# A long convolution with a gated mix on one Trainium2 core: the inverse stage in eight 32x64 array tiles, two channels side by side in the first exchange, and a rewritten order

## The chip, the cores and the metric

The kernel runs on one core of a Trainium2 chip. The core has a matrix engine (TensorE, PE in the rows), a vector engine (VectorE, DVE), a scalar engine (ScalarE, ACT), a general engine (GpSimd, POOL) and an engine that only issues transfers here (SyncE, SP). Each engine works through its own instructions in program order and waits at semaphores for the others. PE writes to PSUM, from which DVE and ACT read; all other working data lie in SBUF.

The metric is device time in microseconds (us). The kernel before takes 198.89 us, the median of 3 runs between 198.06 and 199.80.

## What is computed

The input is one sequence of 2048 tokens with 512 channels, all in fp32. Two branches are mixed by a gate per token:

```python
k_shift = sum(k_pad[:, t:t + S, :] * shift_k[:, ks - 1 - t] for t in range(4))   # 4 taps per channel
kv = k_shift * v
y = irfft(rfft(kv padded to 2S) * rfft(ssm_k padded to 2S))[:S] + kv * ssm_D     # long causal convolution
a = q * y
r = q @ w_r; idx = top2(r)                                                       # two routed tokens
ffn = (silu(q[idx] @ w_gate) * (q[idx] @ w_up)) @ w_down * sigmoid(r[idx])
b = q; b[idx] += ffn
g = sigmoid((q * gate_w).sum(-1))
out = g * a + (1 - g) * b
```

## The kernel before

The 512 channels are worked in four chunks `c` of 128. For each chunk the convolution is a transform of length 2048 = 64 x 32, done by matmuls against constant tables, and these are the stages:

- `taps(c, x)`: the four taps of a quarter of the chunk's tokens, multiplied and added in SBUF tile `acc` (4 buffers). ACT makes the first product. The other three are done on DVE for the four blocks of chunk 0 (`TAPS_DVE`), elsewhere by a product on ACT (`tap`) and an addition on POOL.
- `T(c, x)`: four PE transposes into PSUM tile `ps` (one buffer), and a DVE product with `v` into `kv`.
- `A(c, b)` and `C(c, b)`: matmuls with `w1` over 64 positions, of the filter `hN` and of `kv`, into a PSUM tile `p2`. There are three `p2` buffers, of two banks each, which `A`, `C`, `S` and `I` share. `exchange` (line 149) then has DVE transpose the 128x1024 tile in 32x32 blocks out of PSUM into `e`. A chunk has eight of these. `skip` (`D` in the order) adds one row to `hN` on POOL before `A`.
- `S(c, u)`, eight a chunk: 16 matmuls with `w2` into `p2`, on eight array tiles of 64 rows by 32 columns; ACT copies one half to `g`; DVE makes the products `y1` and `y2`; after every second `S`, POOL adds or subtracts their halves. `y1` and `y2` have two buffers.
- `I(c, u)`, four a chunk: the inverse with `w3`, four matmuls of 64x128 tiles and 512 columns in two row halves, into one `p2`; two ACT copies of 128x512 put it into `f`.
- `X(c, i)`, four a chunk: DVE transposes `f` in place in 32x32 blocks, when all of the chunk's `I` are there.
- `J(c, mb)`, four a chunk: eight matmuls with `vv`, into `ps`, or into `p2` for the last chunk; then the gate (`gcol`, `omg`), four small instructions on ACT or DVE as `GATE` says; then a product with `q` (`qN`, 4 buffers) on POOL or DVE; then the store.
- `G`: the steps of `ffn`, that is the gate and router over all tokens, the search for two tokens, and their feed-forward matmuls, whose weights stream through `wff` (two buffers). `Z(c)` scatters the routed result with an addition, issued by POOL.

Each fp32 matmul is recorded as two instructions. The names `L...` in the order are loads, all issued by SP. The string `ORDER` sets everything: every name in it runs its function up to the next `yield`, so the string is the program order of all engines at once.

Of the kernel before, what the change touches and what calls it, by code (L numbers as in the profile page):

```python
# [519 lines left out]
```

## Time and profile before

| | before |
|---|---|
| median of 3 runs | 198.89 us |
| the profiled execution | 198.09 us |
| its span, first to last instruction | 196.1 us |
| PE busy | 146.9 us (75%) |
| DVE busy | 150.6 us (77%) |
| ACT busy | 93.3 us (48%) |
| POOL busy | 115.4 us (59%) |
| moved by DMA | 39.77 MB, mean 203 GB/s |

The profile is of one execution. Busy time is the union of an engine's instructions, without issue and semaphore time, and a group's mean is the length of one instruction, of which several can overlap on PE. PE's weight loads (PEld) have their own column. The idle time before a group is put down to what released its last instruction.

### The profile page before, as it was taken

To read this page: it belongs to the slowest core of one execution; us is meant where nothing else is said; L and a number is where in the kernel's file an instruction comes from. 1 tells how busy PE (TensorE), PEld (TensorE's weight loads), DVE (VectorE), ACT (ScalarE), POOL (GpSimd) and SP (SyncE) were. 2 spreads that over 40 slices of the span, in tenths; PEclk is the share of its full clock that TensorE was granted. 3 is DMA by queue.
4 is the path that set the end of the run, shared out by engine and by line. 5 is a ranking of instruction groups with operands and counts; after the bars stand their busy time and mean duration, and the time that the engine had idled before them with its cause. 6 is when DMAs were issued, how large, how long until landed. Compare 5 with 4: busy or idle time off the path is not lost. (4 is left out here: it accounts for less than half of the span.)

```text
span 196.1 us, 4562 instructions
## 1 busy us (share of the span) xinstructions
PE 146.9 (75%) x1822; PEld 70.3 (36%) x1822; DVE 150.6 (77%) x179; ACT 93.3 (48%) x178; POOL 115.4 (59%) x107
## 2 busy tenths in 40 slices
PE   0028748788978797998897999899989997974700
PEld 0014222334523234542443534444356452423600
DVE  0198799997889998999769879988999845047540
ACT  0611655265597245753395672432556555660500
POOL 0021889159899276974595898460613992931662
PEclk9999999999999999999999999999999999998885
DMA  5999994858699300079578464675640757786140
GB/s 133 366 324 273 341 341 166 295 196 310 210 322 349 119 0 4 3 246 336 194 271 278 159 230 142 208 232 174 187 149 24 261 140 242 184 275 209 60 159 0
DMA packets 16473, 39.77 MB, mean 203 GB/s; under 512 B 2361, under 2 KB 2883, under 8 KB 16325
## 3 DMA queue, kind: packets, MB, share of 16 engines
q1 hardware_dynamic: 16292, 39.48, 60.7%
q8 instruction: 14, 0.23, 0.5%
q0 software_dynamic: 160, 0.01, 0.2%
q14 instruction: 7, 0.05, 0.1%
HBM read 35.28 MB, written 4.20 MB: 201 GB/s over the span
## 5 line engine op out<-in xcount | busy, mean ns | idle before, releaser
L149 DVE STREAM_TRANSPOSE e<-p 128x1024 f32<-128x1024 f32 x32 | 62.8, 2041 | 5.6 <-PE p L199 2.9
L229 POOL TENSOR_TENSOR y<-y 128x512 f32<-128x512 f32 x32 | 40.3, 1282 | 21.6 <-DVE y L222 21.3
L176 POOL TENSOR_TENSOR acc<-acc,tap 128x512 f32<-128x512 f32 x36 | 45.9, 1280 | 11.1 <-ACT tap L174 6.7
L212 PE MATMUL p<-e,w 64*32 64x256 f32 x1024 | 32.7, 380 | 5.9 <-DVE e L149 5.1
L241 PE MATMUL p<-y,w 64*128 64x512 f32 x128 | 31.8, 611 | 3.2 <-POOL y L229 1.4
L246 ACT ACTIVATE f<-p 128x512 f32<-128x512 f32 x32 | 18.1, 625 | 25.2 <-PE p L241 25.1
L276 POOL TENSOR_TENSOR qN<-oA,qN 128x512 f32<-128x512 f32 x14 | 17.9, 1278 | 20.3 <-ACT oA L271 16.2
L217 ACT ACTIVATE g<-p 128x512 f32<-128x512 f32 x32 | 18.9, 598 | 22.5 <-PE p L212 15.0
L222 DVE TENSOR_TENSOR y<-p,g 128x512 f32<-128x512 f32 x32 | 21.8, 682 | 9.3 <-PE p L241 4.1
L174 ACT ACTIVATE tap<-kT,shk 128x512 f32<-128x512 f32 x36 | 25.4, 718 | 4.3 <-POOL acc L176 4.1
L212 PEld LDWEIGHTS p<-e,w 64*32 64x32 f32 x1024 | 17.7, 106 | 19.8 <-DVE e L149 8.5
L254 DVE STREAM_TRANSPOSE f<-f 128x1024 f32<-128x1024 f32 x16 | 19.3, 1223 | 7.0 <-ACT f L246 7.0
L185 PE MATMUL ps<-ident,acc 128*128 128x128 f32 x64 | 11.4, 305 | 16.1 <-DVE acc L171 13.5
L271 ACT ACTIVATE oA<-ps,omg,gcol 128x128 f32<-128x128 f32 x48 | 18.0, 460 | 11.4 <-PE ps L263 9.1
L223 DVE TENSOR_TENSOR y<-p,g 128x512 f32<-128x512 f32 x32 | 21.8, 683 | 1.0 <-POOL y L229 0.7
L199 PE MATMUL p<-kv,w 64*128 64x512 f32 x64 | 17.3, 640 | 5.1 <-DVE e L149 2.1
L158 PE MATMUL p<-hN,w 64*128 64x512 f32 x64 | 18.0, 661 | 1.8 <-DVE e L149 1.2
L241 PEld LDWEIGHTS p<-y,w 64*128 64x128 f32 x128 | 11.5, 186 | 18.4 <-issue 9.3
L185 PEld LDWEIGHTS ps<-ident,acc 128*128 128x128 f32 x64 | 7.3, 150 | 25.6 <-DVE acc L171 13.5
L167 ACT ACTIVATE acc<-kT,shk 128x512 f32<-128x512 f32 x16 | 11.2, 719 | 10.9 <-DMA kT<-in_kT_dram 10.8
L171 DVE SCALAR_TENSOR_TENSOR acc<-kT,shk,acc 128x512 f32<-128x512 f32 x12 | 8.7, 748 | 9.1 <-ACT acc L167 8.9
L140 POOL TENSOR_TENSOR hN<-hN,drow 1x32 f32<-1x32 f32 x16 | 5.2, 324 | 15.0 <-DMA hN<-in_hN_dram 14.4
(63 smaller groups left out, 117.0 us busy)
## 6 DMA issues: line engine op xcount, KB each, us to landing
vN<-in_vN_dram SPq DMA_DIRECT2D x16, 256.0 KB, 5.2
hN<-in_hN_dram SPq DMA_DIRECT2D x8, 512.0 KB, 5.3
wff<-in_qT_dram SPq DMA_DIRECT2D x8, 512.0 KB, 5.6
qN<-in_qN_dram SPq DMA_DIRECT2D x16, 256.0 KB, 3.4
out_dram<-qN SPq DMA_DIRECT2D x16, 256.0 KB, 3.8
wff<-in_wg_dram SPq DMA_DIRECT2D x8, 448.0 KB, 4.1
wff<-in_wu_dram SPq DMA_DIRECT2D x8, 448.0 KB, 4.6
wff<-in_wd_dram SPq DMA_DIRECT2D x8, 448.0 KB, 5.6
```

What stands on the lines that cost most here:

```text
L149: nc.vector.transpose(ee[c][:, i, b * 8:(b + 1) * 8].rearrange("p d k e -> p d e k"), p)
L174: nc.scalar.activation(s, w[j], AF.Copy, scale=shk[:, c, j:j + 1])
L176: nc.gpsimd.tensor_add(acc, acc, s)
L185: nc.tensor.transpose(p[:, i], acc[:, i * 128:(i + 1) * 128], ident)
L212: nc.tensor.matmul(p[32 * j:32 * j + 32, b, ri].rearrange("p i d -> p (i d)"), w2[r, 4 * u + j, 32 * ri:32 * ri + 32], e[r, :, 4 * u + j, ...
L217: nc.scalar.activation(g, p[:, :, :, 0], AF.Copy)
L222: nc.vector.tensor_mul(y1[:, u % 2], p[:, :, :, 1], g)
L223: nc.vector.tensor_mul(y2[:, u % 2], p[:, :, ::-1, 1], g)
L229: nc.gpsimd.tensor_tensor(w[:, :, 0], w[:, :, 0], w[:, :, 1], op=op)
L241: nc.tensor.matmul(p[:, j], w3[r, w], y[r, :, ri], start=(n == 0), stop=(n == len(parts) - 1))
L246: nc.scalar.activation(ff[c][:, :, o:o + 4].rearrange("p d k e -> p k d e"), p[:, j].rearrange("p k (d e) -> p k d e", e=2), AF.Copy)
L254: nc.vector.transpose(w, w)
```

## The change

`I` now does the work of two old units: 16 matmuls on eight array tiles of 32 rows by 64 columns, each with 512 columns, into two `p2` at once (four banks), and two ACT copies of 128x1024. The table `w3` shrinks with it, and `vv` is permuted on the host to fit. `e` is laid out with two channels side by side (8 bytes from one value of a block's row to the next) where it had four (16 bytes). `y1` and `y2` get a third buffer.

In the last chunk a new step `Q` makes `q * g` and `q * (1 - g)` ahead on ACT (32 small instructions), so that `J` ends with one DVE product out of PSUM and one POOL addition. The other chunks' gates all go to ACT. `acc`, the gate's output and `Q` now share one set of four buffers. Tap block (0, 3) moves from DVE to ACT and POOL. The order is new throughout.

```diff
-P = dict(h=2, k=2, v=3, q=4, wff=2, acc=4, g=2, y=2, o=1)
-TAPS_DVE = {(0, 0), (0, 1), (0, 2), (0, 3)}
-GATE = [["AP"] * 4, ["AP"] * 4, ["AP"] * 4, ["AP", "DD", "AP", "DD"]]
+P = dict(h=2, k=2, v=3, q=4, wff=2, acc=4, g=2, y=3, o=1)
+TAPS = ["DDDA", "AAAA", "AAAA", "AAAA"]
...
-L5 L3 Lk L0 Lk L8 taps0.0 taps0.1 taps0.0 taps0.0 Lk taps0.0 Lk Lv L2 Lv taps0.1 taps0.1 taps0.2 L1 L4 taps0.1 L9
+Lk L0 Lv Lk L4 Lh taps0.0 taps0.0 taps0.0 taps0.1 L3 L1 taps0.0 D0 Lk Lk L2 Lv taps0.1 T0.0 taps0.1 A0.1 taps0.2
...
-    w3 = const.tile([128, 3, 128], F32, name="w3")
+    w3 = const.tile([128, 2, 64], F32, name="w3")
...
-            ee[c] = epool.tile([128, 2, DC // 4, 32, 4], F32, name="e")
+            ee[c] = epool.tile([128, 2, DC // 2, 32, 2], F32, name="e")
...
-        nc.vector.transpose(ee[c][:, i, b * 8:(b + 1) * 8].rearrange("p d k e -> p d e k"), p)
+        nc.vector.transpose(ee[c][:, i, b * 16:(b + 1) * 16].rearrange("p d k e -> p d e k"), p)
...
-        p = ps2.tile([128, 2, 4, DC], F32, name="p2")
-        y1, y2 = (y.rearrange("p t b r d -> p (t b) r d") for y in ys.pop((c, u)))
-        parts = [(y1, 0, 0), (y2, 0, 2)] if (c, u) in SUMS else [(y1, 0, 0), (y1, 1, 1), (y2, 0, 2), (y2, 1, 2)]
-        for n, (y, ri, w) in enumerate(parts):
-            for j in range(2):
-                r = slice(64 * j, 64 * j + 64)
-                nc.tensor.matmul(p[:, j], w3[r, w], y[r, :, ri], start=(n == 0), stop=(n == len(parts) - 1))
+        y = [tuple(z.rearrange("p t b r d -> p (t b) r d") for z in ys.pop((c, 2 * u + w))) for w in range(2)]
+        pp = [ps2.tile([128, 2, 4, DC], F32, name="p2") for _ in range(2)]
+        for n in range(2):
+            for kp in range(4):
+                for h in range(2):
+                    r = slice(32 * kp, 32 * kp + 32)
+                    nc.tensor.matmul(pp[kp // 2][64 * h:64 * h + 64, kp % 2], w3[r, n], y[(h - kp) % 2][n][r, :, 0],
+                                     start=(n == 0), stop=(n == 1), skip_group_check=True)
...
+    def Q(c, mb):
+
+        qn = qst.get(4 * c + mb)
+        qgs[mb] = qg = wk.tile([128, 4, DC], F32, name="acc", bufs=P["acc"])
+        for i in range(4):
+            nc.scalar.activation(qg[:, i], qn[:, i], AF.Copy, scale=gcol[:, mb * 4 + i:mb * 4 + i + 1])
+        yield
+        for i in range(4):
+            nc.scalar.activation(qn[:, i], qn[:, i], AF.Copy, scale=omg[:, mb * 4 + i:mb * 4 + i + 1])
...
+        if c == NC - 1:
+            qg = qgs[mb]
+            nc.vector.tensor_mul(qg, p, qg)
+            yield
+            qn = qst.get(4 * c + mb)
+            nc.gpsimd.tensor_add(qn, qg, qn)
```

Three places show how the order moves instructions. The first is DVE from its first instruction on, before the first `S`. L171 and L166 are the tap multiplies of chunk 0, L187 and L184 the products of `T`, L149 and L144 the transposes of `exchange`. Before:

```order
L171 SCALAR_TENSOR_TENSOR acc<-kT,shk,acc 128x512 x8
L187 TENSOR_TENSOR kv<-ps,vN 128x4x64x2
L171 SCALAR_TENSOR_TENSOR acc<-kT,shk,acc 128x512
L187 TENSOR_TENSOR kv<-ps,vN 128x4x64x2
L171 SCALAR_TENSOR_TENSOR acc<-kT,shk,acc 128x512 x3
L149 STREAM_TRANSPOSE e<-p_167 128x8x4x32
L149 STREAM_TRANSPOSE e<-p_155 128x8x4x32
L187 TENSOR_TENSOR kv<-ps,vN 128x4x64x2
L149 STREAM_TRANSPOSE e<-p_197 128x8x4x32
L187 TENSOR_TENSOR kv<-ps,vN 128x4x64x2
L149 STREAM_TRANSPOSE e<-p_164 128x8x4x32
L149 STREAM_TRANSPOSE e<-p_219 128x8x4x32
```

And after, where DVE has 9 tap multiplies instead of 12 in the same stretch and the first transpose stands between the products of `T`:

```order
L166 SCALAR_TENSOR_TENSOR acc<-kT,shk,acc 128x512 x6
L184 TENSOR_TENSOR kv<-ps,vN 128x4x64x2
L166 SCALAR_TENSOR_TENSOR acc<-kT,shk,acc 128x512
L184 TENSOR_TENSOR kv<-ps,vN 128x4x64x2
L166 SCALAR_TENSOR_TENSOR acc<-kT,shk,acc 128x512 x2
L144 STREAM_TRANSPOSE e<-p_126 128x16x2x32
L184 TENSOR_TENSOR kv<-ps,vN 128x4x64x2
L144 STREAM_TRANSPOSE e<-p_172 128x16x2x32
L144 STREAM_TRANSPOSE e<-p_192 128x16x2x32
L184 TENSOR_TENSOR kv<-ps,vN 128x4x64x2
L144 STREAM_TRANSPOSE e<-p_189 128x16x2x32
L144 STREAM_TRANSPOSE e<-p_218 128x16x2x32
```

The second place is PE around an inverse in the middle of the program. L212 is `S`, L356 a small router matmul, L241 the inverse into one `p`, L373 a feed-forward block, L158 `A`. Before:

```order
L212 MATMUL p_814<-e,w_80 32x256 x16
L356 MATMUL pf<-wrg,xsT 32x32 x4
L241 MATMUL p_855<-y_756,w_81 128x512 x2
L241 MATMUL p_855<-y_757,w_81 128x512 x2
L373 MATMUL pf<-wff,xsT 32x224 x8
L158 MATMUL p_876<-hN,w_78 128x512 x2
```

And after, where L361, L182 (the transposes of `T`) and L368 follow the last `S` and the inverse (L238, its first half) goes to two `p` in turn and takes two `y` of each kind:

```order
L208 MATMUL p_700<-e,w_80 32x256 x16
L361 MATMUL pf<-ident,pe_645 128x128 x4
L182 MATMUL ps<-ident,acc 128x128 x4
L368 MATMUL pf<-wrg,xsT 32x32 x4
L238 MATMUL p_763<-y_441,w_81 64x512
L238 MATMUL p_763<-y_654,w_81 64x512 x2
L238 MATMUL p_763<-y_441,w_81 64x512
L238 MATMUL p_764<-y_441,w_81 64x512
L238 MATMUL p_764<-y_654,w_81 64x512 x2
L238 MATMUL p_764<-y_441,w_81 64x512
```

The third place is the end of DVE's program. L222 and L223 (after: L218 and L219) are the products of the last `S`, L393 and L398 (after: L405 and L410) two steps of the feed-forward result, L254 and L252 the transposes `X`. Before:

```order
L222 TENSOR_TENSOR y_1843<-p_1762,g 128x512
L223 TENSOR_TENSOR y_1844<-p_1762,g 128x512
L254 STREAM_TRANSPOSE f<-f 128x16x2x32
L393 COPY pe_1903<-pf 128x512
L254 STREAM_TRANSPOSE f<-f 128x16x2x32 x3
L398 TENSOR_SCALAR pe_1911<-pf,fac 2x512
L273 TENSOR_SCALAR oD<-p_1934,gcol,omg 128x128 x4
L276 TENSOR_TENSOR qN<-oD,qN 128x512
L273 TENSOR_SCALAR oD<-p_1951,gcol,omg 128x128 x4
L276 TENSOR_TENSOR qN<-oD,qN 128x512
```

And after, where both feed-forward steps stand ahead of the four `X`, and the gates and products become the four products L277:

```order
L218 TENSOR_TENSOR y_1896<-p_1877,g 128x512
L219 TENSOR_TENSOR y_1897<-p_1877,g 128x512
L405 COPY pe_1933<-pf 128x512
L410 TENSOR_SCALAR pe_1964<-pf,fac 2x512
L252 STREAM_TRANSPOSE f<-f 128x16x2x32 x4
L277 TENSOR_TENSOR acc<-p_2012,acc 128x512
L277 TENSOR_TENSOR acc<-p_2003,acc 128x512
L277 TENSOR_TENSOR acc<-p_2041,acc 128x512
L277 TENSOR_TENSOR acc<-p_2027,acc 128x512
```

On PE the last two `S` before the last inverse are followed by one `J`, one block of the down projection and the whole inverse; before, three inverses, three `J` and two blocks of the down projection stood behind the last `S`.

## Rows read from the trace of the kernel before

**Rows 1.** The page's head and part 1: busy us (share of the span) xinstructions.

```profile
span 196.1 us, 4562 instructions
...
PE 146.9 (75%) x1822; PEld 70.3 (36%) x1822; DVE 150.6 (77%) x179; ACT 93.3 (48%) x178; POOL 115.4 (59%) x107
```

**Rows 2.** Windows of three stages: start:end and length, busy us (xcount), PEclk, DMA share, GB/s.

```profile
20.00:160.00 140.00, 120.91 (x1612) 56.24 (x1616) 127.24 (x145) 74.50 (x140) 95.66 (x86) 1.00 0.60 203
160.00:196.10 36.10, 20.40 (x210) 11.11 (x188) 13.53 (x20) 13.65 (x34) 17.53 (x14) 0.86 0.52 161
```

**Rows 3.** Windows cut at the first S, the last S and the last J.

```profile
0.00:37.00 37.00, 17.58 (x76) 6.76 (x76) 26.16 (x25) 13.29 (x19) 15.97 (x22) 1.00 0.82 273
37.00:161.30 124.30, 110.20 (x1594) 53.16 (x1594) 110.94 (x135) 67.67 (x130) 83.24 (x73) 1.00 0.58 193
```

**Rows 4.** Groups by line: names, shapes, count, busy us, mean ns, idle before and releasers.

```profile
L149 DVE STREAM_TRANSPOSE e<-p 128x1024 f32<-128x1024 f32 x32 | 62.8, 2041 | 5.6 <-PE p L199 2.9 <-PE p L158 2.7
L176 POOL TENSOR_TENSOR acc<-acc,tap 128x512 f32<-128x512 f32 x36 | 45.9, 1280 | 11.1 <-ACT tap L174 6.7 <-issue 3.3
...
L212 PE MATMUL p<-e,w 64*32 64x256 f32 x1024 | 32.7, 380 | 5.9 <-DVE e L149 5.1 <-DVE y L223 0.6
L241 PE MATMUL p<-y,w 64*128 64x512 f32 x128 | 31.8, 611 | 3.2 <-POOL y L229 1.4 <-DVE e L149 0.8 <-DVE where L297 0.8
...
L254 DVE STREAM_TRANSPOSE f<-f 128x1024 f32<-128x1024 f32 x16 | 19.3, 1223 | 7.0 <-ACT f L246 7.0
...
L263 PE MATMUL ps<-f,vv 128*64 128x128 f32 x192 | 13.2, 277 | 0.7 <-ACT oA L271 0.7
```

**Rows 5.** Timeline of ACT, then DVE, at the start: start us, us, what.

```profile
6.82 1.28 ACT L167 ACT_TABLE_LOAD   x1 [6.82 <-DMA shk<-in_shk_dram]
...
8.87 6.01 DVE L171 SCALAR_TENSOR_TENSOR acc<-kT,shk,acc 128x512 f32<-128x512 f32 x8 [8.87 <-ACT acc L167]
...
27.53 13.19 DVE L149 STREAM_TRANSPOSE e<-p 128x1024 f32<-128x1024 f32 x7
...
41.13 0.70 DVE L222 TENSOR_TENSOR y<-p,g 128x512 f32<-128x512 f32 x1
41.73 0.71 DVE L223 TENSOR_TENSOR y<-p,g 128x512 f32<-128x512 f32 x1
```

**Rows 6.** Timeline of PE: the first S, the last S, the last J.

```profile
37.03 1.10 PE L212 MATMUL p<-e,w 64*32 64x256 f32 x32
...
159.40 1.96 PE L212 MATMUL p<-e,w 64*32 64x256 f32 x64
...
179.69 5.26 PE L263 MATMUL p<-f,vv 128*64 128x128 f32 x64 [2.48 <-DVE f L254]
```

**Rows 7.** Timeline of all engines, 158 to 197 us.

```profile
163.60 0.69 DVE L222 TENSOR_TENSOR y<-p,g 128x512 f32<-128x512 f32 x1 [4.08 <-PE p L241]
...
168.15 2.49 POOL L229 TENSOR_TENSOR y<-y 128x512 f32<-128x512 f32 x2
...
168.41 3.70 PE L241 MATMUL p<-y,w 64*128 64x512 f32 x16
...
169.97 3.28 ACT L246 ACTIVATE f<-p 128x512 f32<-128x512 f32 x6
...
173.26 1.50 ACT L271 ACTIVATE oA<-ps,omg,gcol 128x128 f32<-128x128 f32 x4
...
175.44 0.69 DVE L393 COPY pe<-pf 128x512 f32<-128x512 f32 x1 [0.91 <-PE pf L390]
176.05 3.49 DVE L254 STREAM_TRANSPOSE f<-f 128x1024 f32<-128x1024 f32 x3
```

**Rows 8.** Windows of the last J: the column after the five engines is PEclk.

```profile
179.60:181.00 1.40, 1.31 (x13) 1.34 (x14) 0.56 (x1) 0.00 (x0) 0.53 (x1) 0.50 0.44 88
```

**Rows 9.** The chain that ended last, in order of time: start us, us, what.

```profile
186.93 1.58 DVE qN L276
...
192.07 1.58 POOLq L514
```

More of the change, by code (lines that the diff above doesn't have):

```diff
@@ L181, in T @@
             kvs[c] = wk.tile([128, DC // 2, 16, 2], F32, name="kv", bufs=1)
+        to = kvs[c][:, :, 4 * x:4 * x + 4, :]
+        v = vst.get(4 * c + x)
         acc = accs.pop((c, x))
@@ L224, in S @@
         mark(("y", c, u // 2))
-        if (c, u // 2) in SUMS and u % 2 == 1:
+        if u % 2 == 1:
             yield
@@ L266, in J @@
         yield
-        o = ld.tile([128, 4, DC], F32, name="o" + GATE[c][mb][0], bufs=1)
-        for i in range(4):
-            m = mb * 4 + i
-            if GATE[c][mb][0] == "A":
-                nc.scalar.activation(o[:, i], p[:, i], AF.Identity, bias=omg[:, m:m + 1], scale=gcol[:, m:m + 1])
-            else:
-                nc.vector.tensor_scalar(o[:, i], p[:, i], gcol[:, m:m + 1], omg[:, m:m + 1], op0=ALU.mult, op1=ALU.add)
-        yield
-        qn = qst.get(4 * c + mb)
-        (nc.gpsimd if GATE[c][mb][1] == "P" else nc.vector).tensor_mul(qn, o, qn)
+        if c == NC - 1:
[4 more added lines that the diff above has]
+            nc.gpsimd.tensor_add(qn, qg, qn)
+        else:
+            o = wk.tile([128, 4, DC], F32, name="acc", bufs=P["acc"])
+            for i in range(4):
+                m = mb * 4 + i
+                nc.scalar.activation(o[:, i], p[:, i], AF.Identity, bias=omg[:, m:m + 1], scale=gcol[:, m:m + 1])
+            yield
+            qn = qst.get(4 * c + mb)
+            nc.gpsimd.tensor_mul(qn, o, qn)
         yield
@@ L382, in ffn @@
             nc.tensor.transpose(ph[:FS, s4], sg[:, s4 * FS:(s4 + 1) * FS], ident)
-        hT = small([128, 4, 128], "hT")
+        hT = small([128, 512], "pe0").rearrange("p (s f) -> p s f", s=4)
         nc.vector.tensor_copy(hT[:FS], ph[:FS])
@@ L413, in mixed_kernel @@
         work[f"L{n}"] = fetch(dst, src)
+    for mb in range(4):
+        work[f"Q{NC - 1}.{mb}"] = Q(NC - 1, mb)
     for c in range(NC):
@@ L419, in mixed_kernel @@
             work[f"S{c}.{u}"] = S(c, u)
+        for u in range(2):
+            work[f"I{c}.{u}"] = I(c, u)
         for u in range(4):
-            for f in (A, C, I, J, T, X, taps):
+            for f in (A, C, J, T, X, taps):
                 work[f"{f.__name__}{c}.{u}"] = f(c, u)
@@ L446, in _shape_constants @@
     c, s = np.cos(t), np.sin(t)
-    w3 = np.zeros((2, 2, 32, 3, 2, 2, 32))
-    for h in range(2):
-        for z in range(2):
-            w3[h, z, :, 0, z] = np.stack([c, s], 1)
-            w3[h, z, :, 1, z] = np.stack([-c, -s], 1)
-            w3[h, z, :, 2, z] = np.stack([-s, c], 1)
+    w3 = np.stack([np.stack([c, s], 1), np.stack([-s, c], 1)], 1).reshape(32, 2, 64)
     ph = 2 * np.pi * (k1 + 0.25)[:, None, None] * (n2[None, :, None] + N2 * n1[None, None, :]) / S
-    k1p = np.array([[32 * b + 4 * g + 2 * r + z for r in range(2) for g in range(8) for b in range(2)]
-                    for z in range(2)])
+    k1p = np.array([[32 * b + 16 * u + 8 * ((h - kp) % 2) + 4 * t + kp for u in range(2) for kp in range(4)
+                     for t in range(2) for b in range(2)] for h in range(2)])
     v = np.stack([np.cos(ph)[k1p], -np.sin(ph)[k1p]], 1).reshape(128, 32, 64) / S
```

67 lines of the change are left out of this document (32 added, 35 removed).

## The prediction, made before the changed kernel ran

> **What bounds it now.** I read the page's totals first. PE is busy 146.9 us and DVE 150.6 us of a 196.1 us span; POOL and ACT have 115.4 and 93.3 [rows 1]. Shares over a whole span hide its stages, so the windows come next: between 20 and 160 us DVE is busy 127.24 of 140 us (91%) and PE 120.91 (86%), but after 160 us, in 36.1 us, PE is busy 20.40 and DVE 13.53 [rows 2]. So the middle is bound by two engines that take turns in waiting for each other, and the end is a chain in which one engine works at a time. The groups by line then say what fills the two busy engines: 62.8 us of DVE is the transpose `exchange` out of PSUM, 2041 ns for 128x1024, and 31.8 us of PE is the inverse `I` [rows 4]. The other DVE transpose of the same size, `X`, takes 1223 ns [rows 4]. Last I read the timeline of the start and of the end: the first matmul of `S` begins at 37.03, the last `S` ends at 159.40 + 1.96 = 161.36, and the last four `J` begin at 179.69 [rows 6]. That gives three stretches: 37.0 us of start, 124.3 of middle, 34.7 of end.
>
> **The inverse.** Before, one `I` is 4 matmuls, each recorded as two instructions: x128 in 16 units, busy 31.8 us, so 1.99 us a unit and 248 ns an instruction of 512 columns while two array tiles work side by side [rows 4]. After, one `I` does the work of two, in 16 matmuls or 32 instructions of 512 columns, on eight tiles of 32x64. The trace has no tiles of 32 rows. The nearest row is `S`, which also runs on eight tiles (64x32): 32.7 us for 1024 instructions of 256 columns, 31.9 ns each [rows 4]. Twice the columns makes 63.9 ns, times 32 is 2.04 us a unit, 16.3 us for eight units: 31.8 - 16.3 = 15.5 us less PE. The bad bound is that no more tiles run together than in `I` today: 256 x 248 ns = 63.5 us, 32 us more. I take the `S` row, since it too has eight different moving operands at once, and half of its tiles differ in their rows. [...]
>
> **The transposes out of PSUM.** `e` changes from four channels side by side to two, so that the 32 values of a row that one block writes lie 8 bytes apart instead of 16. `f`, on which `X` works, already has that layout, and its transpose of equal size costs 1223 ns against 2041. If the step of the write is the cause, 32 transposes save 0.818 us each, 26.2 us of DVE. If reading PSUM is the cause they save nothing. For the first speaks that a DVE multiply out of PSUM of 512 elements takes 0.70 us and follows its neighbour after 0.60 us, about what `X` needs per 512 reading SBUF, 3.49 / 6 = 0.58 [rows 5, 7]; so PSUM as a source is not slow. I take 1223 ns. [...] `S` will read `e` in pieces of two instead of four. `J` reads `f` in twos now: its 128 columns take 277 ns, while the 256 columns of `S` in pieces of four take 380 [rows 4]. The shorter pieces cost nothing that shows, so I cost this at nothing.
>
> **Small moves.** One block of taps goes from DVE to ACT and POOL: three multiplies of 0.75 us (6.01 for 8 [rows 5]) leave DVE, three additions of 1.28 us come to POOL [rows 4], three copies to ACT. In the last chunk DVE's gates and products become four multiplies of 0.70, a small saving at the very end that I don't count; POOL does four additions instead of two products, +2.6 us; ACT loses 8 gates and gets the 32 small ones of `Q`, at 1.50 us for four [rows 7] 12 us. ACT's 16 evictions of 1024 replace 32 of 512, at no more in all. Totals: PE 146.9 - 15.5 = 131.4; DVE 150.6 - 26.2 - 2.2 = 122.2; POOL 115.4 + 3.8 + 2.6 = 121.8; ACT below 108. PE becomes the tallest.
>
> **Start.** The order on DVE before the first `S` was 12 tap multiplies, 4 of `T`, and 8 transposes; now it is 9, 4 and 8. At pitches of 0.75, 0.60 and 1.88 us (13.19 for 7) before, and 1.16 (3.49 for 3 of `X`) after [rows 5, 7]: 9.0 + 2.4 + 15.0 = 26.4 against 6.8 + 2.4 + 9.3 = 18.5. That is 7.9 us. The half of `w2`, the first and largest load, moves behind `C0`; ACT's start at 6.82 waited for `shk` behind it [rows 5], worth perhaps 1 us more, but the late `w2` can cost that again. I take -8, between -3 (loads limit, when the DMA engines are already 82% busy in the first 37 us [rows 3]) and -10.
>
> **Middle.** From first to last `S` PE is busy 110.20 of 124.3 us, idle 14.1 [rows 3]. 13 old inverses lie in it and 7 new ones will; two more `J` (1.1 each), one more block of the down projection (1.05) and one of the router (1.1) move in by the order: 110.2 - 25.9 + 14.3 + 4.3 = 102.9. DVE's 110.94 loses 24 transposes, 19.6, so it no longer co-binds. The idle time may fall for that. But `I` now takes two of the three `p2` buffers at once and its matmuls wait until the `S` before has been drained; the two `y` multiplies at 0.60 us pitch are 1.2 us, and other matmuls that use `ps` or `pf` stand in between half the time, so 0.6 x 7 = 4.2 us. Behind the waiting `I` stand the next `S` and `A` on PE, and DVE waits for those. With 14.1 kept: 102.9 + 14.1 + 4.2 = 121.2, which is -3.1. The bounds: -12 when the idle time halves without the second engine and no buffer wait appears; +12 when every `I` waits for a whole drain (0.6 + 1.2) and the next `S` for a first eviction (1.0).
>
> **End.** Before, from the last `S` to the last `J`s is 179.69 - 161.36 = 18.3 us: `y` waited 4.08 us for the old `I` to free its buffers, the POOL sums began at 168.15 behind two products, two inverses ran 3.70, evictions ended at 173.25, and `X` was interrupted by the copy at 175.44 [rows 7]. After, the third `y` buffer takes the first wait away and the copy stands ahead of all four `X`: `g` and the `y`s to +2.2, sums to +4.2, the second half of `I` 1.3 to +5.5, two evictions to +7.5, `X` 4.65 to +12.2. That is -6.1. `Q` stands on ACT between, one ahead of the last evictions (inside the wait for the sums), the others under `X` and `J`. [...] Store, scatter and close from 188.5 on stay 7.6 [rows 9]. I take -6, between -2 and -8.
>
> **Sum.** 8 + 3.1 + 6 = 17.1; the profiled run takes 198.09 with its 196.1 span, so 181.0. The median of the runs shown, 198.89, is 0.8 above that run; I forecast **181**.
>
> **Rivals.** *Row tiles don't run eight at once* (the other side). Place: every `I` on PE. Each further microsecond per unit costs 8. Four at once is 4.1 us a unit, +16.4: 197. Two at once, 8 us: 229. It turns slower by over 1% at 4.5 us a unit, about three tiles at once. For it: no row of 32-row tiles. Against: `S` and two row tiles in `I` both overlap. Chance 0.10. *The layout doesn't speed the transposes.* DVE stays the middle's bound: start -2, middle 0, end -6, so 190. For it: only `X` has the fast layout, and it reads SBUF. Chance 0.12. *Buffers and order eat the gain*: the middle's +12 bound and a start held by loads, -3: 198 + 12 - 3 - 6 = 201, and 190 when half of it comes. For it: one `I` now needs two of three buffers, POOL, DVE and PE are within 10%. Chance 0.10.
>
> **Numbers.** The forecast's case has 0.68, with its own 173 to 189. To leave out two in ten the range reaches over the slow transposes and half-eaten gains: 173 to 193. A measurement of this kernel tells about 1% from no change. Faster: 0.68 + 0.11 + 0.04 + 0.01 = 0.84. Same: 0.01 + 0.03 + 0.02 = 0.06. Slower: 0.03 + 0.07 = 0.10.
>
> **What would show it.** The inverse's group near 16 us of PE; `exchange` at 1.2 us; first `S` near 29 us; PE above 85% between first and last `S` with DVE near 75%; last `S` to last `J`s near 12 us. Wrong if `exchange` stays at 2 us, if the inverse takes over 3 us a unit, or if PE's idle time in the middle grows past 20 us.

## The result, and the profile after

| | before | after |
|---|---|---|
| median of 4 runs, side by side | 198.47 us | 189.69 us |
| ratio, 95% interval | | 0.9535 [0.9427, 0.9644] |
| profiled execution, its span | 198.09, 196.1 us | 190.25, 188.1 us |
| PE busy | 146.9 us (75%) | 149.3 us (79%) |
| DVE busy | 150.6 us (77%) | 127.8 us (68%) |
| ACT, POOL busy | 93.3, 115.4 us | 102.8, 123.2 us |

The change makes the kernel 4.7% faster. Ratios and their intervals leave out executions more than 1.5% above the fastest of their kernel, medians don't, so here and below a ratio need not be the quotient of two medians. The forecast was 181.0 us with a range of 173 to 193, so the direction and the range hold, and the forecast itself was 8.7 us too low. The first view cuts the span at the first `S`, the end of the last `S` and the last group of `J`, as [rows 3] did: stretch and length, busy us (xcount) of PE, PEld, DVE, ACT and POOL, then the granted clock of PE, DMA share, GB/s.

```profile
0.00:30.27 30.27, 18.33 (x68) 7.59 (x68) 20.50 (x22) 13.73 (x19) 15.57 (x21) 0.94 0.83 272
30.27:159.40 129.13, 119.07 (x1764) 52.88 (x1764) 96.47 (x136) 74.71 (x130) 92.30 (x80) 0.93 0.67 221
159.40:171.64 12.24, 6.00 (x60) 1.68 (x59) 8.29 (x10) 10.96 (x29) 7.73 (x7) 0.91 0.45 155
171.64:188.10 16.46, 5.90 (x64) 5.66 (x64) 2.58 (x4) 3.36 (x12) 7.58 (x6) 0.60 0.18 64
```

The start is 6.8 us shorter than the 37.03 of before (forecast 8). From the end of the last `S` to the last `J` it is 12.24 us (forecast 12.2), and the whole end is 28.7 against 34.7 us, 6.0 shorter (forecast 6). The middle is 4.8 us **longer** than its 124.3 of before, where 3.1 less were forecast. So 7.9 of the 9.1 us by which this execution's span missed (188.1 for a forecast 179.0) lie in the middle. There PE is busy 119.07 us instead of the 102.9 of the forecast, and idle 10.06 instead of 18.3. Nearly all of that idle time is in a few waits: 4.17 us for `wu`, 4.43 in four waits for the router, 0.61 for the gate, 0.58 for a `p2` buffer. The waits of `S` for `e`, 5.1 us before [rows 4], are gone. The granted clock, 1.00 in the middle before, is 0.93.

The groups by line, to be read against [rows 4]: line, engine, names, shapes, count, busy us, mean ns, idle before.

```profile
L208 PE MATMUL p<-e,w 64*32 64x256 f32 x1024 | 42.1, 465 | 0.6 <-ACT f L244 0.6
L144 DVE STREAM_TRANSPOSE e<-p 128x1024 f32<-128x1024 f32 x32 | 39.0, 1247 | 7.9 <-PE p L153 5.2 <-PE p L195 2.6
L238 PE MATMUL p<-y,w 32*64 32x512 f32 x256 | 20.0, 704 | 0.0
```

`exchange` fell from 2041 to 1247 ns as forecast. The inverse fell from 31.8 to 20.0 us. `S` (now L208), which nobody touched, rose from 32.7 to 42.1 us: that alone takes back 9.4 of PE's gain. The timeline of PE in the middle shows where more of it went (start us, length, line, what, and idle time before it with its releaser):

```profile
51.51 0.30 PE L307 MATMUL pf<-ident,m 128*128 128x128 f32 x1 [0.94 <-DVE m L304]
53.26 0.48 PE L307 MATMUL pf<-ident,m 128*128 128x128 f32 x1 [1.45 <-DVE m L304]
53.66 3.84 PE L238 MATMUL p<-y,w 32*64 32x512 f32 x32
...
68.87 3.82 PE L238 MATMUL p<-y,w 32*64 32x512 f32 x32
...
81.71 1.97 PE L238 MATMUL p<-y,w 32*64 32x512 f32 x32
...
106.15 0.98 PE L385 MATMUL pf<-wff,xsT 128*32 128x224 f32 x8 [4.17 <-DMA wff<-in_wu_dram]
107.05 5.03 PE L208 MATMUL p<-e,w 64*32 64x256 f32 x96
```

An inverse unit at a granted clock of 1.00, as from 81.71 to 83.68, takes 1.97 us. Two of the eight took 3.84 and 3.82. Short waits stand before both (0.94 and 1.45 us for the router's maxima `m`, and 1.37 us for the gathered rows at 66.04), and the windows of these units give a granted clock of 0.61 and 0.50:

```profile
53.66:57.50 3.84, 3.84 (x34) 1.28 (x34) 3.74 (x6) 0.41 (x2) 3.84 (x4) 0.61 0.51 198
...
68.87:72.69 3.82, 3.82 (x38) 1.25 (x40) 2.11 (x5) 2.06 (x5) 2.11 (x2) 0.50 1.01 373
...
107.05:112.08 5.03, 5.03 (x104) 2.37 (x104) 1.95 (x4) 2.47 (x4) 1.34 (x1) 0.58 0.80 233
```

The last row is the `S` of 96 instructions behind the 4.17 us wait for `wu`, at a granted clock of 0.58. At clock 1.00, from 75.19 on, such a row takes 3.67.

### The profile page after: what moved, and what is told of

It reads as the page before. It is cut to its first block, busy times and chain, and to the rows that moved or that the text cites. A ratio compares the mean times of both kernels' runs of the same rounds, so it can differ in the third digit from the quotient of the medians.

```text
span 188.1 us, 4801 instructions
## 1 busy us (share of the span) xinstructions
PE 149.3 (79%) x1950; PEld 67.8 (36%) x1950; DVE 127.8 (68%) x170; ACT 102.8 (55%) x189; POOL 123.2 (65%) x112
## 4 chain that ended last, share of the span: by engine, by line
PE 59%; DMA 17%; DVE 9%; ACT 6%; issue 4%; SPq 2%; POOL 1%; POOLq 1%; DVEq 0%; ACTq 0%
PE p L208 15%; PE p L153 8%; PE p L195 7%; PE ps L271 6%; PE p L238 6%; PE pf L385 4%; DMA wff<-in_qT_dram 4%; DMA wff<-in_wd_dram 3%; PE ps L182 3%; DMA wff<-in_wu_dram 3%; PE p L271 3%; DMA ident<-in_ident_dram 3%; DVE e L144 2%; DMA pe<-in_qrow_dram,ti 2%; PE pf L402 2%
## 5 line engine op out<-in xcount | busy, mean ns | idle before, releaser
L171 POOL TENSOR_TENSOR acc<-acc,tap 128x512 f32<-128x512 f32 x39 | 51.4, 1325 | 16.9 <-ACT tap L169 15.7
L144 DVE STREAM_TRANSPOSE e<-p 128x1024 f32<-128x1024 f32 x32 | 39.0, 1247 | 7.9 <-PE p L153 5.2
L208 PE MATMUL p<-e,w 64*32 64x256 f32 x1024 | 42.1, 465 | 0.6 <-ACT f L244 0.6
L169 ACT ACTIVATE tap<-kT,shk 128x512 f32<-128x512 f32 x39 | 28.5, 741 | 7.4 <-POOL acc L171 7.4
L218 DVE TENSOR_TENSOR y<-p,g 128x512 f32<-128x512 f32 x32 | 22.0, 686 | 13.6 <-ACT g L213 13.2
L208 PEld LDWEIGHTS p<-e,w 64*32 64x32 f32 x1024 | 18.3, 114 | 20.7 <-issue 5.2
L285 ACT ACTIVATE acc<-ps,omg,gcol 128x128 f32<-128x128 f32 x48 | 18.1, 460 | 13.5 <-PE ps L271 13.5
L288 POOL TENSOR_TENSOR qN<-acc,qN 128x512 f32<-128x512 f32 x12 | 15.7, 1317 | 13.0 <-ACT acc L285 12.9
L219 DVE TENSOR_TENSOR y<-p,g 128x512 f32<-128x512 f32 x32 | 21.9, 683 | 0.0
L252 DVE STREAM_TRANSPOSE f<-f 128x1024 f32<-128x1024 f32 x16 | 19.4, 1256 | 3.5 <-ACT f L244 3.5
L153 PE MATMUL p<-hN,w 64*128 64x512 f32 x64 | 20.5, 732 | 0.8 <-issue 0.7
L182 PE MATMUL ps<-ident,acc 128*128 128x128 f32 x64 | 12.0, 318 | 11.1 <-DMA ident<-in_ident_dram 9.2
L244 ACT ACTIVATE f<-p 128x1024 f32<-128x1024 f32 x16 | 16.1, 1056 | 7.9 <-PE p L238 7.9
L238 PE MATMUL p<-y,w 32*64 32x512 f32 x256 | 20.0, 704 | 0.0
L195 PE MATMUL p<-kv,w 64*128 64x512 f32 x64 | 16.4, 629 | 0.1
L182 PEld LDWEIGHTS ps<-ident,acc 128*128 128x128 f32 x64 | 7.9, 159 | 22.0 <-DVE acc L166 9.1
L184 DVE TENSOR_TENSOR kv<-ps,vN 128x512 f32<-128x512 f32 x16 | 11.6, 724 | 5.1 <-PE ps L182 5.1
L271 PE MATMUL ps<-f,vv 128*64 128x128 f32 x192 | 13.3, 277 | 0.6 <-ACT acc L285 0.6
```

The source lines that it names most:

```text
L144: nc.vector.transpose(ee[c][:, i, b * 16:(b + 1) * 16].rearrange("p d k e -> p d e k"), p)
L153: nc.tensor.matmul(p[:, j], w1[r], hs.get(t)[r, 16 * (b % 2):16 * (b % 2) + 16], start=True, stop=True)
L169: nc.scalar.activation(s, w[j], AF.Copy, scale=shk[:, c, j:j + 1])
L171: nc.gpsimd.tensor_add(acc, acc, s)
L182: nc.tensor.transpose(p[:, i], acc[:, i * 128:(i + 1) * 128], ident)
L195: nc.tensor.matmul(p[:, par].rearrange("p (d e) m -> p d e m", e=2), w1[r], x[r], start=True, stop=True)
```

## The experiments

### Which part of the change made the gain

Three kernels change one number, how many channels stand side by side in `e`, and nothing else: the kernel before with two (label b_e2), the changed kernel with four (e4) and with one (e1).

```diff
+EC = [2, 2, 2, 2]          # b_e2;  [4, 4, 4, 4] in e4;  [1, 1, 1, 1] in e1
-            ee[c] = epool.tile([128, 2, DC // 4, 32, 4], F32, name="e")
+            ee[c] = epool.tile([128, 2, DC * 32], F32, name="e").rearrange(
+                "p i (d k e) -> p i d k e", k=32, e=EC[c])
```

Expected of b_e2:

> The kernel before with only e laid out with two channels side by side. Theory (pieces of two): exchange falls to 1.25 us and DVE to about 125, S rises to about 42 us and PE to about 156; PE then binds and the time stays within 3% of before, 193 to 199. Rival (S is slower through the new order): S stays at 32.7 us, and the time falls to 185 to 190.

Expected of e4:

> The changed kernel with only e put back to four channels side by side. Theory (S is slower because it reads e in pieces of two): S falls back to about 32.7 us busy (1.1 us for one, 1.96 for two), while exchange rises to 2.04 us, so DVE goes from 128 to about 153 us busy; the time ends near the old one, 195 to 200. Rival (S is slower through its neighbours in the new order or the lower clock): S stays near 42 us although e has its old layout; exchange rises all the same.

Expected of e1:

> The changed kernel with each channel of e by itself, so that exchange writes 32 neighbouring values and S reads single ones. Theory (S pays for each piece it reads): with twice the pieces S goes from 1.25 us to 1.9 to 2.6 us, 60 to 80 us busy in all; exchange stays at 1.2 us, since it is already at full speed; the time passes 205. Rival (S is slower through order and clock): S stays near 42 us and the time near 190.

Measured: b_e2 187.44 us, ratio 0.9479 [0.9369, 0.9590]; e4 198.24 us, 1.0003 [0.9942, 1.0064]; e1 233.74 us in a single execution. The groups of `S` and of `exchange`, for b_e2, then e4, then e1 (the line numbers are each kernel's own):

```profile
L214 PE MATMUL p<-e,w 64*32 64x256 f32 x1024 | 40.7, 451 | 0.2 <-DVE y L225 0.2
L151 DVE STREAM_TRANSPOSE e<-p 128x1024 f32<-128x1024 f32 x32 | 39.3, 1255 | 10.1 <-PE p L201 5.6 <-PE p L160 4.4
L243 PE MATMUL p<-y,w 64*128 64x512 f32 x128 | 31.0, 605 | 0.2
```

```profile
L146 DVE STREAM_TRANSPOSE e<-p 128x1024 f32<-128x1024 f32 x32 | 63.5, 2058 | 5.1 <-PE p L155 3.9 <-PE p L197 1.0
L210 PE MATMUL p<-e,w 64*32 64x256 f32 x1024 | 34.7, 395 | 4.7 <-DVE e L146 3.9 <-ACT f L246 0.6
```

```profile
L210 PE MATMUL p<-e,w 64*32 64x256 f32 x1024 | 91.5, 876 | 0.6 <-ACT f L246 0.6
L146 DVE STREAM_TRANSPOSE e<-p 128x1024 f32<-128x1024 f32 x32 | 38.4, 1230 | 9.0 <-PE p L155 6.3 <-PE p L197 2.4
```

Of the expectations, e4's came: `S` went down to 34.7 us, so what slows it goes with the layout and not with its neighbours in the new order. In b_e2 `S` rose and `exchange` fell as the theory had it, but its time, 193 to 199, did not come: 187.44 lies in the range of the rival, whose reason (`S` stays at 32.7 us) is refuted. The theory had not reckoned with how little PE would wait, as the windows below show. In e1 `S` went well beyond the theory's 60 to 80 us.

Two things follow. First, the layout by itself gives the whole gain, as far as these intervals tell: the old kernel with this one edit stands at 0.9479, the whole change at 0.9535, and their intervals overlap; without it the rest of the change gives 1.0003, nothing that shows (DVE, with `exchange` back at 63.5 us, is then as busy as PE again, 148.6 and 148.9 us). Second, the layout has a price on PE that the prediction set at nothing. `S` costs 32.7 to 34.7 us with pieces of four fp32 in its moving operand, 40.7 to 42.1 with two and 91.5 with one, while the transpose gains only from four to two (2058, 1255, 1230 ns). Two is the best of the three. With the width of the pieces the step from one to the next changes too (128, 64, 32 values); no run parts the two.

Why the rest gives nothing net is read from b_e2 beside the changed kernel. The same cut at its first and last `S`:

```profile
0.00:34.33 34.33, 18.48 (x77) 7.42 (x77) 21.77 (x26) 12.77 (x19) 13.59 (x19) 1.00 0.86 285
34.33:153.56 119.23, 116.23 (x1595) 54.11 (x1596) 97.90 (x134) 70.93 (x132) 87.73 (x76) 1.00 0.62 207
153.56:185.70 32.14, 19.01 (x154) 10.50 (x154) 12.66 (x20) 11.83 (x29) 15.69 (x12) 0.84 0.54 165
```

With the old inverse and order, PE is busy 116.23 of 119.23 us at a granted clock of 1.00: it became the bound, and it hardly waits. From b_e2's span of 185.7 to the 188.1 of the changed kernel, the inverse takes 11.0 us off PE (31.0 to 20.0), the other PE instructions take 6.6 more (153.73 - 31.0 against 149.30 - 20.0), and PE idles 6.8 more (32.0 against 38.8): -11.0 + 6.6 + 6.8 = +2.4. By stage the idle time falls 3.9 us at the start, where the new order brings the first `S` forward, and rises 7.1 in the middle and 3.7 at the end. So the inverse's gain of PE time is there, and by this account it is spent on PE's waits and on slower matmuls. The account sets one profile against one, and a second profile of the changed kernel has a span of 186.8 us. No run has the old inverse in the new order on this layout, so what the inverse and the order do apart is not shown.

### Does PE's work still set the middle

The changed kernel, with the 16 matmuls of each inverse done twice (the second time over the first, with the same result):

```diff
-        for n in range(2):
+        for n in (0, 1, 0, 1):
```

> The changed kernel with every inverse computed twice over in the same banks, 32 more instructions a unit; the result is the same. Prices PE time at the inverse: at the measured 2.0 us a unit it adds 16 us of PE. Theory (PE binds the middle, nothing else does): the time rises by 13 to 17 us, to 203 to 207. Rival (DVE, POOL and loads bind as much): it rises by less than 8 us, and PE's idle time in the middle falls instead.

Measured: 202.02 us, 1.0225 [1.0129, 1.0320], 12.3 us above the changed kernel, a little under the theory's 13 to 17 and far from the rival's 8. PE's busy time rose by 13.3 (162.6), the span by 11.9. Work added to PE passes nearly whole into the time, so PE does bind. That a microsecond taken off PE is worth as much, this run does not show; it may come back as waiting.

### The load of `wu`

In the changed kernel PE waits 4.17 us for a piece of `wu` at 106.15. SP's timeline and its own waits tell why:

```profile
99.57 0.33 SPq L82 DMA_DIRECT2D vN<-in_vN_dram  x1
100.00 0.37 SPq L82 DMA_DIRECT2D wff<-in_wu_dram  x1
```

```profile
SPq L82 <- DVE kv L184: 12.1, 3, 7.5
```

SP issued the two in program order, `vN` at 99.57 and `wu` at 100.00. The load of `vN` waited up to 7.5 us for DVE's product that still read its buffer, and `wu` stood behind it, though its own buffer was free (with the edit below the same piece is issued by 90.9). The matmul that needs it began 6.1 us after its issue. The edit moves one token (label hoist):

```diff
-taps3.0 Lh Lv taps3.2 C2.0 A2.0 Lw T3.1
+taps3.0 Lw Lh Lv taps3.2 C2.0 A2.0 T3.1
```

> The changed kernel with one token of its order moved: the load of wu's next piece is issued on SP ahead of chunk 3's filter load and of chunk 2's value load, instead of two loads behind them. In the changed kernel the value load waited 7.5 us on SP for the last product T that reads its old buffer, the wu load stood behind it, and TensorE then waited 4.17 us for wu (106.15) and took 5.03 us for the 96 matmuls of the next S at half clock. Theory (a queue's order costs the middle that wait and the cold stretch behind it): the wait goes, the S takes 3.7, the time falls by 4 to 5.6 us, to 184 to 186. Rival (the filter or the value load is now what is late, or what TensorE did in that time was hidden anyway): 188 to 190, the wait found at another line.

Measured: 186.23 us, 0.9507 [0.9271, 0.9743], just above the theory's 184 to 186. The interval is too wide to set it apart from the changed kernel by the medians; the trace does. The wait is gone from its place, with smaller ones of 1.26 and 0.67 us a little later:

```profile
101.69 1.37 PE L208 MATMUL p<-e,w 64*32 64x256 f32 x32
104.32 2.52 PE L208 MATMUL p<-e,w 64*32 64x256 f32 x64 [1.26 <-ACT f L244]
...
108.02 1.37 PE L208 MATMUL p<-e,w 64*32 64x256 f32 x32 [0.67 <-DVE y L219]
```

First to last `S` takes 125.38 us, against 129.13 in the first profile of the changed kernel and 127.08 in a second one (label after2, below, where the wait came in three parts of 2.74, 1.67 and 0.90 us, and the `S` of 96 behind the first took 3.67, its length at clock 1.00). The wait goes as the theory says. Its worth is 1.7 to 3.8 us here, in place of 4 to 5.6, and the run best, below, with the same edit and a middle of 126.57, puts it lower still.

### The router's waits, filled

The two slow inverse units stand behind short waits for the router. Label warm puts matmuls that compute nothing into those waits, four of 128x128 ahead of each transpose of a maximum and two of 128x512 ahead of the gathered rows' transpose (the second edit is left out below); hoist_warm has this and the moved load.

```diff
         pr = psf.tile([128, 128], F32, name="pf")
+        for _ in range(4):
+            nc.tensor.matmul(pr, ident, ident, start=True, stop=True, skip_group_check=True)
...
```

> The changed kernel with more matmuls that compute nothing: four 128x128 ones before each of the four transposes of the routing's maxima, two 128x512 ones before the transpose of the gathered rows, which TensorE does while it would wait for the maximum or the gather (the result is overwritten, nothing else is changed). In the changed kernel the two inverse units behind such waits took 3.84 and 3.82 us at a granted clock of 0.5 to 0.6, the others 1.97 to 2.2. Theory (the short waits drop the clock and the units behind them pay): those two units fall to about 2.0 us, the time falls by 3 to 4 us to 186 to 187. Rival (the clock falls whatever these waits hold, or the time at half clock is hidden): the units stay near 3.8, or the time stays at 189 to 191.

> Both edits together: the wu load moved ahead on SP, and the matmuls that fill the routing's waits. Theory (the middle is TensorE's own work plus two kinds of waits with cold stretches, and they add): 180 to 183 us. Rival (one hides behind the other): 184 to 187.

Measured: warm 190.09 us, 0.9618 [0.9246, 0.9989]; hoist_warm 188.05 us, 0.9501 [0.9096, 0.9907], above both its theory (180 to 183) and its rival (184 to 187). PE in warm, then in hoist_warm:

```profile
53.16 1.16 PE L308 MATMUL pf<-ident 128*128 128x128 f32 x8 [0.38 <-DVE col L311]
54.36 2.47 PE L238 MATMUL p<-y,w 32*64 32x512 f32 x32
...
70.03 4.42 PE L238 MATMUL p<-y,w 32*64 32x512 f32 x32
```

```profile
53.98 2.47 PE L238 MATMUL p<-y,w 32*64 32x512 f32 x32
...
70.06 2.73 PE L238 MATMUL p<-y,w 32*64 32x512 f32 x32
```

The first unit fell from 3.84 to 2.47 us, at a granted clock of 1.00 in that window, so the waits before it were what slowed it; the 0.5 us that it keeps over 1.97 stay unexplained. The second stayed slow in warm (4.42, clock 0.61), but in hoist_warm it took 2.73, between two `S` of 96 instructions (from 61.41 and from 74.81) of 3.67 each, their length at clock 1.00. And still the time did not fall: first to last `S` takes 127.45 us in hoist_warm, against 125.38 with the moved load alone. The filling has a cost of its own: it writes to the same PSUM tile `pf`, so it waited for DVE's last read of it (0.60 us at 51.14 and 0.38 at 52.79 in hoist_warm), filled only part of the wait and delayed the transposes behind it, for which DVE waits: the first begins at 52.13 instead of 51.47 with the moved load alone, the last at 59.33 instead of 58.82. A link from clock to unit is shown. That removing the slow clock pays is not shown: with this filling it did not.

Hoist_warm also prices the clock, by an estimate. Its middle took every `S` of 32, 64 and 96 instructions in 1.36 to 1.38, 2.51 to 2.52 and 3.67 us, and none of its inverse units took over 2.73; I take it as a middle at clock 1.00. PE is busy there for 120.44 us, 6.6 of them with the filling (4.6 and 2.0 by line), which leaves 113.8 us for the changed kernel's own matmuls, for the 119.07 that they took.

### The router's waits, ordered away

Label spread has the moved load, and another sequence for some forty steps between 48 and 68 us, with no instruction added (one place of it is shown): matmuls of `S` and of the inverse stand between the router's transposes, which stood nearly back to back. Label spread_tail adds six 128x512 matmuls that compute nothing ahead of the last `J`, in PE's wait for `X`. The changed kernel ran again beside them (after2).

```diff
-C1.2 C1.1 G G A1.3 G taps2.2 Lv Lw A1.3 G I0.0 C1.0 G T2.1 G
+C1.2 C1.1 C1.0 G G A1.3 S0.6 A1.3 S0.6 G I0.0 taps2.2 Lv Lw S0.6 G I0.0 T2.1
...
         p = pool.tile([128, 4, DC], F32, name=name)
+        if (c, mb) == (NC - 1, 1):
+            for _ in range(6):
+                nc.tensor.matmul(p.rearrange("p a b -> p (a b)"), ident, w2[:, 0:8].rearrange("p a b -> p (a b)"),
+                                 start=True, stop=True, skip_group_check=True)
```

> The changed kernel itself, beside the two runs that follow, so that they can be set against it on one chip: 188 to 191 us by every theory.

> The changed kernel with the wu load ahead on SP as in the run of that edit, and some forty steps of its order between 48 and 68 us written in another sequence: the matmuls of two S, of the first inverse and of one more S stand between the transposes of the routing's maxima, which stood nearly back to back, and the second inverse stands ahead of the gathered rows' transpose instead of behind it. No instruction is added or left out. In the run of the moved load TensorE waited 0.90, 1.46, 0.47 and 1.11 us there and the inverse units behind took 4.19 and 3.49 us. Theory (these waits, and the low clock behind them, are what the change's order cost the middle): both units fall to about 2.0 us, the waits to under 1 us in all, and the span falls by 4 to 6 us against 184.3 of that run, to 178 to 180; a median of 180 to 182. Rival (routing comes later and the FFN's loads and products pay for it, or POOL's taps are what the middle goes by): 184 to 188.

> The same, with six 128x512 matmuls that compute nothing ahead of the last product group J, in the 5.84 us in which TensorE waits for the transposes X; their sums are overwritten. In the changed kernel the last J took 5.91 us at a granted clock of 0.50. Theory (the clock fell in that wait and the tail pays it at the end): the 64 matmuls take 4.4 to 4.8 us, the end falls by 1 to 1.5 us. Rival (the clock is low at the end whatever TensorE does there, or the product's end is hidden behind DVE's and POOL's): the end stays within 0.4 us.

Measured: after2 188.73 us, 0.9560 [0.9455, 0.9665]; spread 190.24 us, 0.9614 [0.9291, 0.9937]; spread_tail 188.54 us, 0.9592 [0.9418, 0.9765]. In spread (its inverse is L215, the transposes of `T` L159):

```profile
51.78 2.51 PE L215 MATMUL p<-y,w 32*64 32x512 f32 x32
...
65.98 1.11 PE L159 MATMUL ps<-ident,acc 128*128 128x128 f32 x4 [4.78 <-POOL acc L148]
67.02 3.18 PE L215 MATMUL p<-y,w 32*64 32x512 f32 x32
```

The router's waits fell to 0.74 us in all and the first unit to 2.51, but PE now waits 4.78 us for the tap additions on POOL. POOL's timeline shows what held them:

```profile
62.23 1.03 POOL L328 DMA_INDIRECT pe<-in_qrow_dram,ti  x1 [1.42 <-DVE y L195]
63.29 2.63 POOL L148 TENSOR_TENSOR acc<-acc,tap 128x512 f32<-128x512 f32 x2
```

The gather is issued by POOL, which stood idle 1.42 us before it. DVE's steps for the tokens' numbers were through at 61.59; the profile names the product behind them (L195, to 62.19) as what ended that wait. The two tap additions stand behind the gather, and the second unit, behind PE's wait for them, stayed at 3.18 us (the granted clock from 66 to 72 us is 0.73). The theory on this middle fell. Its rival holds in its mechanism, POOL's taps, though not in its number: 190.24 is above its 184 to 188 too. With the router's waits gone, the next thing late was POOL's queue, 66% busy over the span. No run mends that as well, so what the middle could then give stays open.

At the end the theory holds, and by more than its 1 to 1.5 us: from the last `S` on, spread takes 28.60 us and spread_tail 26.82. The last `J` in spread, then in spread_tail:

```profile
171.04 5.68 PE L248 MATMUL p<-f,vv 128*64 128x128 f32 x64 [5.84 <-ACT qN L240]
```

```profile
170.45 3.96 PE L252 MATMUL p<-f,vv 128*64 128x128 f32 x64 [0.42 <-DVE f L229]
```

The same 64 matmuls take 1.7 us less when PE has been busy in the 5.84 us before them. In spread their granted clock is 0.64; in the changed kernel it is 0.62 (0.50 up to 175.00, then 0.78), and with the six matmuls ahead it is 1.00 in the run best, below, for 3.95 us.

### The inverse in the old order

The kernel before with two channels side by side and the new inverse, in its old order and gate, but with the third buffer of `y1` and `y2` (b_e2_inv). Each new unit stands where the later of its two old ones stood; a few steps had to move where three `p2` didn't suffice.

> The kernel before with the two parts of the change that save work, and with its own order and gate: channels in pairs (two to a position) as in the run of the layout alone (187.44 us; TensorE busy 153.7, 97% of the middle at a granted clock of 1.00), and the inverse in 32x64 tiles over four banks; each new unit stands where the later of its two old ones stood in the order, with a few steps moved behind it where three PSUM buffers did not suffice. Theory (in that middle TensorE binds, and 16 new units at 2.0 us for 32 old at 1.94 take 11 us off it without the waits that the changed kernel's order has): TensorE busy 140 to 143, 176 to 180 us. Rival (less TensorE work only becomes waits and cold clock, whatever the order): TensorE waits 8 us more and the time stays at 184 to 189.

Measured: 202.41 us, 1.0182 [0.9864, 1.0501], against 0.9479 for the layout alone. Its profile is of an execution of 204.08 us, well above the median, so I read only its waits, not its lengths: 3.6 us for `wu`, 3.0 for POOL's sums before an inverse, 1.9 for the down projection's weights, 1.1 for an eviction, where b_e2 has almost none. Three inverses also stop for 0.34 to 1.00 us after their first eight instructions, those for the first of their two `p2`. Neither the theory's 176 to 180 us nor the rival's 184 to 189 came. (The 11 us in the expectation are the 31.0 - 20.0 of the groups; its counts should read 8 new units for 16 old.) But part of these waits are of my own placing (the inverse that waited 3.0 us stands behind an `S` that I moved back), so this run is inconclusive on what the inverse could give in an order made for it. It suggests that the old order, in which PE hardly waited, has no slack for shorter units.

### A faster version

The three edits that the runs had priced, on the changed kernel (label best): the moved load, the six matmuls ahead of the last `J`, and two of the last four additions on DVE.

```diff
-            nc.gpsimd.tensor_add(qn, qg, qn)
+            (nc.vector if mb in (1, 2) else nc.gpsimd).tensor_add(qn, qg, qn)
```

> The changed kernel with three edits that the runs so far priced: wu's load ahead on SP (the middle 3.9 us shorter in that run), six matmuls that compute nothing ahead of the last product group J in the wait for the transposes X (J 3.96 instead of 5.68 us), and two of chunk 3's four last additions on DVE instead of POOL, which stood idle beside it while POOL did four of 1.24 us one after the other. Theory (the three lie one behind the other on the path to the end): the end falls by 2.5 to 3.5 us beside the wait's 3.9, a median of 182.5 to 184.5 us. Rival (POOL's and DVE's additions wait for the same products anyway, so that only J's 1.7 us come): 184.5 to 186.

Measured: 184.02 us, 0.9231 [0.9174, 0.9288], below the intervals of the changed kernel in both of its measurements. Its windows, cut as before, and the last `J` alone:

```profile
28.50:155.07 126.57, 118.20 (x1764) 52.40 (x1764) 97.12 (x136) 75.76 (x132) 94.80 (x82) 0.97 0.68 228
155.07:181.70 26.63, 15.43 (x136) 7.32 (x134) 13.33 (x16) 14.37 (x40) 12.92 (x11) 0.90 0.33 112
167.28:171.23 3.95, 3.95 (x64) 3.49 (x64) 1.75 (x3) 3.46 (x12) 2.33 (x2) 1.00 0.02 1
```

The end is 26.63 us against 28.70 and 29.12 in the two profiles of the changed kernel, so 2.1 to 2.5 of the expected 2.5 to 3.5 came; the middle is 0.5 to 2.6 us shorter, where 3.9 were expected. The first `S` at 28.50, 1.8 us earlier than in the changed kernel, is of no edit's making (the runs with the same start begin it between 28.1 and 30.6), and the single profile owes it some of its lead. So the median came out inside 182.5 to 184.5 with each part a little short.

## Why the prediction was right in direction and too low

**The inverse: right.** 2.04 us a unit was forecast from the row of `S`, and 1.97 is what a unit takes at a granted clock of 1.00. The first rival, that 32-row tiles don't run eight at once, is refuted. A unit of 1.97 us is 32 instructions of 61.6 ns each, against 248 with two tiles [rows 4]. The sum's term of 15.5 came out as 11.8, since two units ran at 0.61 and 0.50 of the clock. (In that rival, 4.5 us a unit is 16.3 / 4.5 = 3.6 tiles at once, not about three.)

**The transposes: right.** 1247 ns for 1223, so 23.8 us of DVE for 26.2. The second rival is refuted: the same transposes out of PSUM took 2058 ns with four channels side by side (e4) and 1247 with two, with the layout of `e` as the only difference.

**"The shorter pieces cost nothing": wrong, and the largest miss.** The step argued from `J`, which reads pieces of two in 277 ns, against 380 for `S`. Those are lengths of overlapping instructions, no rates: by busy time `J` took 68.8 ns for 128 columns on two tiles, 1.07 ns a column and tile, and `S` with pieces of four 1.00, so the rows did not say that pieces of two are free. Why they are dear for `S` is not shown; no run changes the pieces of `J` or the tiles of `S`. The step cost 8.0 us between two middles at a granted clock of 1.00 (40.7 in b_e2, 32.7 before) and 9.4 in the changed kernel.

**The middle: wrong, by 7.9 us.** PE's part was 102.9 forecast, 119.07 measured. Of the 16.2 more, `S` is 9.4; the seven inverse units in this stretch add up to 17.9 us for the 14.3 forecast, 3.6; the rest, 3.2, is in other matmuls (over the whole span the feed-forward group is 9.6 us for 8.1, `A` 20.5 for 18.0, `C` 16.4 for 17.3). Cut the other way, 8.0 is the price of the pieces, about 5.3 the clock by the estimate from hoist_warm, and some 3 the sum had wrong without either. The sum had taken every instruction at the speed of a middle with a granted clock of 1.00, and did not ask whether it would stay there; it came to 0.93. Idle time went the other way, 10.06 for 18.3: DVE, no longer level with PE, gave back more than I dared to count, and the term of 4.2 us for the `p2` buffers came to 0.6. So the terms missed by 16.2 one way and 8.2 the other, and that the median stayed inside the range owes something to luck. None of the prediction's signs of being wrong looked at `S`.

**Start and end: right**, 6.8 for 8 and 6.0 for 6. They carry the direction, since the middle grew. That the layout alone reaches about the same time does not confirm this sum: b_e2 gains 5.1 us in the middle, where the change loses 4.8. The end's term of -6 leaves the last `J` at its 5.26 us of before [rows 6], and no run shows that it stays so. In the changed kernel `J` took 5.90 behind 5.84 us of idle time, at a granted clock of 0.62; before, it took 5.26 behind 2.48 us, at 0.70. In the end two misses cancel: what follows `J` was about as much shorter.

**The third rival**, that buffers and order eat the gain, had the time (190 "when half of it comes") but not the mechanism. What ate it was not the inverse's hold on two of three buffers: PE's idle time before the inverse is 0.0. It was the read of `e`, a load queued behind another on SP, the router's chain, with little of PE's other work between its steps, and the slow clock behind both (0.58 behind the load, 0.61 and 0.50 in the units behind the router).

## What to carry to other kernels

When a layout is changed for the engine that writes it, price it at the engine that reads it, at that reader's own load: the row to take is the reader's own, at two layouts, not another matmul's. When an edit takes work off the engine that binds, list its waits first: each load, gather or small reduction that was hidden by that work can surface. On TensorE the wait for `wu` was paid twice here, once as 4.17 us of idle time and once as matmuls at a granted clock of 0.58 behind it (5.03 us for 3.67 at 1.00). The cheapest repairs found here were one load moved in a queue, and a long wait of TensorE on the final chain filled with matmuls that nobody waits for (the last `J` 3.96 us for 5.68); filling short waits in the middle did not pay (188.05 us with it, 186.23 without).

## What the runs showed of the hardware that I had not expected

**Eight tiles and the width of the pieces they read.** `S` at 4, 2 and 1 fp32 side by side: 32.7 to 34.7, 40.7 to 42.1 and 91.5 us for the same 1024 instructions.

**Slow small steps of DVE in the router's chain end where additions of POOL end.** In the moved-load run, DVE's routing steps of 128x16 elements took 0.83 and 1.00 us, in the reordered run 0.23:

```profile
52.13 0.83 DVE L337 SCALAR_TENSOR_TENSOR cand<-rcol,col,wtrev 128x16 f32<-128x16 f32 x1
...
54.53 1.00 DVE L340 TENSOR_SCALAR cand<-wtrev,where 128x16 f32<-128x16 f32 x1
```

```profile
51.66 2.62 POOL L171 TENSOR_TENSOR acc<-acc,tap 128x512 f32<-128x512 f32 x2 [0.82 <-ACT tap L169]
54.24 2.48 POOL L225 TENSOR_TENSOR y<-y 128x512 f32<-128x512 f32 x2
```

```profile
52.46 0.23 DVE L314 SCALAR_TENSOR_TENSOR cand<-rcol,col,wtrev 128x16 f32<-128x16 f32 x1
```

The slow ones end at 52.96 and 55.53, where POOL's first addition of each pair ends (half of 2.62 after 51.66, half of 2.48 after 54.24); in the reordered run POOL stood idle from 50.60 to 53.06. The same line there took 1.42 us at 56.91, beside an addition of POOL, and ended at 58.33, 0.09 us after it. In the changed kernel three such steps take 0.83, 1.00 and 1.19 us instead of 0.23, 0.23 and 0.17, about 2.4 us more on the router's chain; they end at 53.00, 55.57 and 56.79, and POOL's additions at 53.00, 55.52 and 56.76. No run here moved POOL's work alone, so that these steps wait for POOL is not shown, nor what it is worth in the time.
